# Turned q and k by plain transfers instead of VectorE copies, with the sync queue in program order

## The chip, the cores and the metric

The kernel runs on one core of a Trainium2 chip. The metric is the time of one execution on the device, in microseconds. A core has five engines that run side by side, each with its own in-order queue: TensorE (PE; matrix products, with a separate view of its weight loads, PEld), VectorE (DVE), ScalarE (ACT), GpSimd (POOL) and SyncE (SP). SP computes nothing here: it issues transfers. 16 DMA engines move the data of all queues. On-chip memory is SBUF; TensorE writes to PSUM.

## The reference

Causal attention with a learned decay, on a batch of 8, 8 heads, 576 positions, head size 64, followed by a low-rank mix over positions and a two-layer channel mix.

```python
scores = scale * np.matmul(q, k.transpose(0, 1, 3, 2))
cum = np.cumsum(np.maximum(s, 0.0), axis=-1)
bias = -(cum[:, :, :, None] - cum[:, :, None, :])
scores = np.where(causal, -1000000000.0, scores + np.minimum(bias, 0.0))
attn = softmax(scores)                       # over the last axis
x = np.matmul(attn, v)                       # heads side by side: [8, 576, 512]
h = xt @ U @ V                               # xt: x transposed to [8, 512, 576], rank 32
u = x + h.transpose(0, 2, 1)
out = u + np.maximum(u @ w_ch1, 0.0) @ w_ch2 # 512 -> 2048 -> 512
```

## The kernel before

The 64 heads are worked off as 32 pairs, four pairs to a batch (`NP` = 32, `PB` = 4). The main loop runs over pairs `n` from 8 to 33, with `b, hp = divmod(n, PB)`. One iteration prepares the score operand of pair n+1, computes the scores of pair n (`scores`, L429), and the weighted values of pair n-1 (`values`, L493). Between these steps, `step_fill` puts pieces of the channel mix of earlier tokens (`chanmix`, L662 and L720), so that TensorE always has something to do. In the second pair of each batch (hp = 1) the sequence mix of the batch before runs as well (`seqmix`, L522 to L592): its additions on VectorE (L547) read `xT`, the transposed x of all four pairs of that batch.

The score operand of a pair lies in one of three slots in turn (`slot_of(n)`): 68 partitions, 64 for the head size and four for the decay, and for each of the two heads 576 columns of q and 576 of k. The four decay rows come from DRAM (`rows_of`, two transfers on SP, L302).

For batches 0 to 3, q and k are transposed by TensorE. From batch 4 on (`ZB` = 4) this is done by transfers: `load_pairs` brings q and k in by GpSimd's queue (L121), `turn_pair(n)` (L358) is one DMA transpose on SP from there to a landing place of 128 partitions, 64 for each head of the pair, and `part_pair(n)` copies each half to the slot with VectorE (L366). There are three landing places in turn. `part_pair` has two yields, after each of which the loop puts a piece of fill.

SP issues all transposes and sends in one queue: the turns (L358), the rows (L302), the transposes of x that `values` issues after a pair's second head (`xT`, L510), the transpose of u for the channel mix (`u_sd`, L1026), and the sends of finished quarters of the output (L744). In batches 4 to 7 the planner of the framework chooses SP's order by its own estimates, as it does for VectorE and ScalarE. TensorE's and GpSimd's queues keep the order in which the program was written: the last line of the kernel is `in_program_order(tc, traced, [E.Pool, E.PE])`, which ties each instruction to the one before it on its engine.

An x_sb write (L503) normalises the values of one head; the second of a pair makes that pair's x ready for its transpose. `first_sums` and `total` (L698) and the additions of `outputs_by_quarters` (L734) are the rest of VectorE's work here, with the masks (L373).

Of the kernel before, what the change touches and what calls it, by code (L numbers as in the profile page):

```python
# [19 lines left out]
def in_program_order(tc, first, engines):  # L20

    traced, last = tc.nc.cur_bb.bb.instructions, {}
    for ins in list(traced)[first:]:
        if ins.engine not in engines:
            continue
        prev = last.get(ins.engine)
        if prev is not None:
            tc.add_manual_dep(
                ins,
                prev.name,  # L30
                mybir.DependencyInfo(
                    mybir.DependencyClass.NoSync, mybir.DependencyReason.DATA
                ),
                reason="in_program_order",
            )
        last[ins.engine] = ins
# [3 lines left out]
def kernel(  # L40
# [12 lines left out]
    nc = tc.nc  # L53
    traced = len(nc.cur_bb.bb.instructions)
    E = mybir.EngineType
    B, H, S, D = q.shape
# [7 lines left out]
    NP = BH // 2  # L64
    PB = NP // B
# [5 lines left out]
    ZB = 4  # L71
# [13 lines left out]
    def pwork():  # L85
        return ps_w.tile([128, 512], FP32, tag="w", name="pwork")
# [23 lines left out]
    def by_pairs(b):  # L110
        return qk_sd[b % 2][:TR, :QK].rearrange(
            "p (hp c t two d) -> p hp c t two d", hp=PB, c=2, t=RT, two=2
        )
# [4 lines left out]
    def load_pairs(b):  # L118
        for h in range(H):
            for c, src in enumerate((q, k)):  # L120
                nc.gpsimd.dma_start(  # L121
                    out=by_pairs(b)[:, h // 2, c, :, h % 2, :],
                    in_=src[b, h].rearrange("(t p) d -> p t d", p=TR),
                )
# [51 lines left out]
    def v_slot(b):  # L176
        return v_slots[b % 3 if b < 3 else 2 - b % 2]

    def load_v(b, parts=range(5)):
        vt = v_slot(b)  # L180
        if 0 < b < 3:
            init_v(nc.gpsimd, vt)
        for t in parts:
            rows_t = 128 if t < 4 else 64
            nc.gpsimd.dma_start(  # L185
                out=vt[:rows_t, t, :, 0:D],
                in_=v[b, :, ds(t * 128, rows_t), :].rearrange("h p d -> p h d"),
            )
# [10 lines left out]
    def slot_of(n):  # L199
        return slots[n % NSLOT if n < 2 * PB else (n + 1) % 3]  # L200
# [28 lines left out]
    for n in range(PB):  # L229
        for hh in range(2):  # L230
            nc.sync.dma_start(
                out=slots[n][D:KA, hh, 0 : 2 * S],
                in_=rows[2 * n + hh : 2 * n + hh + 1].rearrange("n r c s -> n r (c s)"),
# [3 lines left out]
    for r, n_r, c in ((0, 3, 1), (3, 1, 0)):  # L237
        nc.sync.dma_start(
            out=rows_hbm[ds(r, n_r), ds(2 * PB, BH - 2 * PB)].rearrange("r n s -> n r s"),
            in_=rows[2 * PB :, ds(r, n_r), c, :],  # L240
# [59 lines left out]
    def rows_of(n):  # L300
        for r, n_r, c in ((0, 3, 1), (3, 1, 0)):
            nc.sync.dma_start(  # L302
                out=slot_of(n)[ds(D + r, n_r), :, ds(c * S, S)],
                in_=rows_hbm[ds(r, n_r), ds(2 * n, 2)],
            )
# [47 lines left out]
    def landing(n):  # L353
        return landings[(n - ZB * PB) % 3]

    def turn_pair(n):
        b, hp = divmod(n, PB)
        nc.sync.dma_start_transpose(  # L358
            out=landing(n).rearrange("p (a m) -> p a m", m=TR),
            in_=by_pairs(b)[:, hp].rearrange("p c t two d -> p (c t two d)"),  # L360
        )

    def part_pair(n):
        rows_of(n)
        for hh in range(2):
            nc.vector.tensor_copy(slot_of(n)[0:D, hh, 0 : 2 * S], landing(n)[ds(hh * D, D)])  # L366
            yield

    def mask(dst, n_tiles, w, on_pool=False):
        if on_pool:  # L370
# [105 lines left out]
    def place(j, i):  # L476
        if i == j:
            return 128 * j if j < 4 else 1536
        return {0: 512, 1: 1024, 2: 1344, 3: 960}[j] + 128 * (i - j - 1)

    def values(n, pT):
        b, hp = divmod(n, PB)
        if hp == 0:
            x_of[b] = work.tile([128, PB, 5, 128], BF16, tag="x_sb", name="x_sb")
            if b >= FT:
                xT_of[b] = work.tile([128, 4, 640], BF16, tag="xT", name="xT", bufs=1)
        x_sb, vt = x_of[b], v_slot(b)
        for hh in range(2):
            h = 2 * hp + hh
            po = pwork()[:, : 5 * (D + 1)].rearrange("p (i d) -> p i d", i=5)  # L490
            for i in range(5):
                for j in range(i + 1):
                    nc.tensor.matmul(  # L493
                        po[:, i, :],
                        lhsT=pT[:, hh, ds(place(j, i), 128)],
                        rhs=vt[:, j, h, :],
                        start=(j == 0),
                        stop=(j == i),
                        skip_group_check=True,
                    )  # L500
            rec = work.tile([128, 5, 1], FP32, tag="rec", name="rec", bufs=4)
            nc.vector.reciprocal(rec, po[:, :, D : D + 1])  # L502
            nc.vector.tensor_tensor(  # L503
                x_sb[:, hp, :, ds(hh * D, D)],
                po[:, :, 0:D],
                rec.to_broadcast([128, 5, D]),
                op=ALU.mult,
            )
            if hh == 1 and b >= FT:
                nc.sync.dma_start_transpose(  # L510
                    out=xT_of[b][:, hp, :].rearrange("p (t m) -> p t m", t=5),
                    in_=x_sb[:, hp, :, :].rearrange("p t d -> p (t d)"),
                )
            yield
# [564 lines left out]
    def step_fill():  # L1079
        pace[0] += pace[1]  # L1080
        if pace[0] < 16:
            return
        pace[0] -= 16
        if NG - 3 in expanded and not ps_tail:
            return
        while fill:
            if next(fill[0], fill) is not fill:
                return
            fill.pop(0)

    def run(gen):
        for _ in gen:
            step_fill()
# [5 lines left out]
    def fill_with(n):  # L1099
        per, pace[1] = pace[1], 16  # L1100
        for _ in range(n):
            step_fill()
        pace[1] = per


    def pT_of(n):
        if n < PB + 3:
            return pTs[n % 2] if n % PB < 2 else pT_early[n % PB - 2]
        return pTs[(n + 1) % 2]

    def step(*gens):
        for gen in gens:
            next(gen, None)
# [85 lines left out]
    def load(b):  # L1199
        alloc_qk(b)  # L1200
        for h in range(0, H, 4 if b == 2 else H):
            load_qk(b, h, 4 if b == 2 else H)
# [38 lines left out]
    pace[1] = 11  # L1241
    for n in range(2 * PB, NP + 2):
        b, hp = divmod(n, PB)
        if hp == 0 and b + 1 < ZB:
            load(b + 1)
        if hp == (1 if b >= ZB else PB - 1) and ZB <= b + 2 < B:
            load_pairs(b + 2)
        if ZB * PB <= n + 3 < NP:
            turn_pair(n + 3)
        mixing = seqmix(b - 1) if hp == 1 and b > FT else iter(())  # L1250
        if b == B:
            fill_with(3)
            for _ in range(3):
                step(mixing)
                fill_with(2)
        if n > 2 * PB and n + 1 < NP:
            for at, _ in enumerate((transposes if n + 1 < ZB * PB else part_pair)(n + 1)):
                step_fill()
                if at == 0:
                    step(mixing)  # L1260
        if 2 * PB + 1 < n < NP:
            for at, _ in enumerate(scores(n, pT_of(n))):
                step_fill()
                if at == 1:
                    step(mixing)
        for _ in mixing:
            fill_with(1)
        if hp == 1 and FT < b < B:
            fill.append(chanmix(b - 1))
            pace[1] = 12 if b < 6 else 10  # L1270
        if 2 * PB < n <= NP:
            run(values(n - 1, pT_of(n - 1)))
        if hp == 0 and 2 <= b < B - 1:
            load_v(b + 1)
    pace[1] = 16
# [36 lines left out]
    while fill:  # L1312
        step_fill()
    in_program_order(tc, traced, [E.Pool, E.PE])


# [28 lines left out]
```

## Time and profile before

| what | value |
|---|---|
| median of 3 runs | 357.68 us (357.58 to 359.25) |
| the profiled execution: its own time | 359.33 us |
| the profiled execution: its span | 357.6 us |
| TensorE busy | 343.6 us (96%) |
| VectorE busy | 264.4 us (74%) |
| L366, copies from a landing place in qk_sd | 20, 475 ns each |
| L366, copies from the landing place `turned` | 12, 478 ns each |
| DMA queue of SP (q1) | 61,640 packets, 22.83 MB, 36.0% of 16 engines' span |
| DMA queue of GpSimd (q0) | 101,744 packets, 18.45 MB, 80.7% |
| granted TensorE clock | 1.00 throughout |

The page shows one profiled execution; the span is what its instructions cover, and the execution's own time is 1.7 us longer. "L547" is line 547 of the kernel. In the timeline a bracket after an instruction tells how long its engine was idle ahead of it and what released it. Matmuls are pipelined, so a group's length is somewhat more than its share of the engine. A packet's time includes the time in which its engine also served another queue, so the shares of the queues can sum to more than one.

### The profile page before, as it was taken

What the parts mean: (1) busy time and instruction counts of PE and PEld (TensorE: products, weight loads), DVE (VectorE), ACT (ScalarE), POOL (GpSimd) and SP (SyncE); (2) the same over time, 40 slices, a digit from 0 to 9 for tenths busy, and PEclk for the clock granted to TensorE, in tenths of its full rate; (3) what the DMA queues carried; (4) which work ended last, traced back from release to release, by engine and by line L of the source; (5) the groups of instructions that cost most, each with busy time, mean ns of one, the idle gap of its engine ahead of it and who ended that gap; (6) DMA issues with size and microseconds to landing.
All of it is one profiled execution on the core that took longest, in us unless ns stands there. A gap on an engine that the chain in (4) does not pass through costs nothing.

```text
span 357.6 us, 9219 instructions
## 1 busy us (share of the span) xinstructions
PE 343.6 (96%) x3770; PEld 247.9 (69%) x3770; DVE 264.4 (74%) x584; ACT 207.6 (58%) x314; POOL 112.6 (31%) x158
## 2 busy tenths in 40 slices
PE   7999999999998999999999997899899999999996
PEld 3685656665587657775678565776588558888885
DVE  8686776779789849883798465983788779676774
ACT  4786965847762577348833874347752554675710
POOL 8897274447356603850366040000000000000000
PEclk9999999999999999999999999999999999999999
DMA  6999999999999999999599999472033525010022
GB/s 100 163 193 203 177 187 121 146 144 97 192 101 171 162 168 88 167 176 159 72 120 160 204 118 90 73 163 57 0 57 83 115 30 120 29 60 31 29 90 88
DMA packets 163713, 42.06 MB, mean 118 GB/s; under 512 B 148312, under 2 KB 162040, under 8 KB 163672
## 3 DMA queue, kind: packets, MB, share of 16 engines
q0 software_dynamic: 101744, 18.45, 80.7%
q1 hardware_dynamic: 61640, 22.83, 36.0%
q8 instruction: 29, 0.48, 0.6%
q10 hardware_dynamic: 288, 0.20, 0.2%
q14 instruction: 12, 0.10, 0.1%
HBM read 37.25 MB, written 9.70 MB: 131 GB/s over the span
## 4 chain that ended last, share of the span: by engine, by line
PE 77%; DVE 12%; ACT 5%; DMA 4%; issue 2%; POOL 0%; DVEq 0%; ACTq 0%; POOLq 0%
PE pwork L662 22%; PE pwork L720 12%; PE quarter L720 9%; PE pscore L429 9%; PE pwork L493 7%; PE parts L950 6%; PE pwork L681 3%; DVE uT L547 3%; DMA xT<-x_sb 2%; ACT pT L447 2%; PE pwork L322 2%; DVE slot L345 2%; DVE o_sb L734 2%; DVE slot L698 2%; ACT hT L1039 1%
## 5 line engine op out<-in xcount | busy, mean ns | idle before, releaser
L662 PE MATMUL pwork<-uT,w_sb 128*128 128x512 bf16 x432 | 106.6, 379 | 1.1 <-ACT hT L1039 0.9
L447 ACT ACTIVATE pT<-pscore 128x1024 bf16<-128x1024 f32 x56 | 56.5, 1031 | 52.7 <-PE pscore L429 52.3
L1039 ACT ACTIVATE hT<-pwork 128x512 bf16<-128x512 f32 x108 | 65.4, 610 | 37.1 <-PE pwork L662 36.3
L662 PEld LDWEIGHTS <-w_sb 128*128 128x128 bf16 x448 | 38.7, 98 | 38.0 <-issue 1.3
L429 PE MATMUL pscore<-slot 68*128 68x320 bf16 (+1 forms) x500 | 55.4, 246 | 0.6 <-ACT hT L447 0.3
L185 POOL DMA_DIRECT2D v_slot<-in_v_dram x40 | 33.8, 860 | 67.9 <-PE pwork L493 57.6
L429 PEld LDWEIGHTS <-slot 68*128 68x128 bf16 x564 | 41.8, 97 | 18.2 <-issue 1.2
L373 DVE TENSOR_TENSOR pT<-pT,keep 128x512 bf16<-128x512 bf16 (+1 forms) x81 | 28.5, 353 | 31.7 <-ACT pT L447 28.7
L720 PEld LDWEIGHTS <-hT 128*128 128x128 bf16 x496 | 46.7, 98 | 7.5 <-issue 0.8
L493 PEld LDWEIGHTS <-pT 128*128 128x128 bf16 x870 | 32.5, 97 | 10.2 <-issue 4.4
L493 PE MATMUL pwork<-v_slot,pT 128*128 128x65 bf16 x870 | 35.8, 193 | 3.8 <-DVE uT L547 3.1
L503 DVE TENSOR_TENSOR x_sb<-pwork,rec 128x320 bf16<-128x320 f32 x64 | 31.2, 489 | 1.5
L459 ACT ACTIVATE pT<-pscore 128x1024 bf16<-128x1024 f32 x29 | 30.4, 1047 | 2.6 <-PE pscore L429 2.4
L720 PE MATMUL pwork<-w_sb,hT 128*128 128x256 bf16 x240 | 30.1, 273 | 0.3 <-DVE o_sb L734 0.3
L345 DVE COPY slot<-pwork 64x576 bf16<-64x576 bf16 x30 | 24.1, 803 | 7.2 <-PE pwork L322 6.8
L121 POOL DMA_DIRECT2D qk_sd<-in_q_dram x32 | 23.8, 743 | 14.0 <-PE pwork L322 4.9
L720 PEld LDWEIGHTS <-slot 128*128 128x128 bf16 x256 | 24.1, 98 | 5.0 <-issue 1.9
L121 POOL DMA_DIRECT2D qk_sd<-in_k_dram x32 | 23.7, 740 | 5.7 <-DMA v_slot<-in_v_dram 1.8
L720 PE MATMUL pwork<-w_sum,slot 128*128 128x256 bf16 x160 | 20.1, 273 | 1.1 <-DVE o_sb L734 1.1
L720 PE MATMUL quarter<-w_sb,hT 128*128 128x256 bf16 x144 | 18.0, 273 | 0.3 <-DVE uT L547 0.3
L681 PE MATMUL pwork<-w_sb,hT 128*128 128x512 bf16 x64 | 16.3, 379 | 0.0
L502 DVE RECIPROCAL rec<-pwork 128x5 f32<-128x5 f32 x64 | 12.0, 189 | 5.4 <-PE pwork L493 5.0
(166 smaller groups left out, 513.7 us busy)
## 6 DMA issues: line engine op xcount, KB each, us to landing
out_dram<-o_sb SPq DMA_DIRECT2D x34, 256.0 KB
v_slot<-in_v_dram POOLq DMA_DIRECT2D x32, 128.0 KB, 7.7
w_sb<-in_moe_w_ch_dram POOLq DMA_DIRECT2D x4, 1024.0 KB, 13.3
qk_sd<-in_q_dram POOLq DMA_DIRECT2D x32, 72.0 KB, 6.0
qk_sd<-in_k_dram POOLq DMA_DIRECT2D x32, 72.0 KB, 5.9
qk_sd<-in_q_dram POOLq DMA_DIRECT2D x4, 288.0 KB, 12.4
qk_sd<-in_k_dram POOLq DMA_DIRECT2D x4, 288.0 KB, 11.5
qk_sd<-in_q_dram POOLq DMA_DIRECT2D x4, 144.0 KB, 5.2
```

The lines of the kernel that those rows point to most:

```text
L121: nc.gpsimd.dma_start(out=by_pairs(b)[:, h // 2, c, :, h % 2, :], in_=src[b, h].rearrange("(t p) d -> p t d", p=TR),)
L185: nc.gpsimd.dma_start(out=vt[:rows_t, t, :, 0:D], in_=v[b, :, ds(t * 128, rows_t), :].rearrange("h p d -> p h d"),)
L345: copies(n, hh, par)(in_turn[:, :, :, :, par], src.rearrange("p c t m -> p c m t"))
L373: nc.vector.tensor_tensor(dst, dst, keep[:, :, 0:w].to_broadcast([128, n_tiles, w]), op=ALU.min)
L429: nc.tensor.matmul(dst, lhsT=slot[0:KA, hh, ds(S + j * 128, 128)], rhs=slot[0:KA, hh, lo:hi], start=True, stop=True,)
L447: nc.scalar.activation(pT[:, hh, 0:1024], near, EXP, scale=scale)
L459: nc.scalar.activation(pT[:, :, 1024:1536], mid.rearrange("p (a b) -> p a b", a=2), EXP, scale=scale)
L493: nc.tensor.matmul(po[:, i, :], lhsT=pT[:, hh, ds(place(j, i), 128)], rhs=vt[:, j, h, :], start=(j == 0), stop=(j == i), skip_group_check= ...
L503: nc.vector.tensor_tensor(x_sb[:, hp, :, ds(hh * D, D)], po[:, :, 0:D], rec.to_broadcast([128, 5, D]), op=ALU.mult,)
L662: nc.tensor.matmul(f1, lhsT=w1_sb[:, kt, ds(nf * 128, 128)], rhs=u[:, kt, :], start=(kt == 0), stop=(kt == 3),)
L720: nc.tensor.matmul(acc[:, i, :], lhsT=a[:, kt, ds(i * 128, 128)], rhs=b[:, kt, :], start=(begin and i == 0 and kt == 0), stop=(kt == HF - ...
L1039: nc.scalar.activation(hT[:, nf, :], f1, RELU)
```

## The change

`part_pair` no longer copies with VectorE: each half of the landing place goes to its half of the slot by a plain transfer on SP, both issued together, and the two yields follow. `turn_pair(n + 3)` is moved from the top of the iteration to below `values(n - 1)`, which is where the transpose of x is issued; in the program it now stands behind that. From the iteration in which n is 12 (batch 3) on, SP's queue keeps the order of the program, as TensorE's and GpSimd's do.

In each iteration SP's queue thus holds, in this order: the rows and the two plain transfers of pair n+1, the sends and the transpose of u that fall into the iteration, the transpose of x of pair n-1, the turn of pair n+3.

```diff
     def part_pair(n):
         rows_of(n)
         for hh in range(2):
-            nc.vector.tensor_copy(slot_of(n)[0:D, hh, 0 : 2 * S], landing(n)[ds(hh * D, D)])
-            yield
+            nc.sync.dma_start(out=slot_of(n)[0:D, hh, 0 : 2 * S], in_=landing(n)[ds(hh * D, D)])
+        yield
+        yield
...
     for n in range(2 * PB, NP + 2):
         b, hp = divmod(n, PB)
+        if n + 4 == ZB * PB:
+            turning = len(nc.cur_bb.bb.instructions)
         if hp == 0 and b + 1 < ZB:
             load(b + 1)
         if hp == (1 if b >= ZB else PB - 1) and ZB <= b + 2 < B:
             load_pairs(b + 2)
-        if ZB * PB <= n + 3 < NP:
-            turn_pair(n + 3)
...
         if 2 * PB < n <= NP:
             run(values(n - 1, pT_of(n - 1)))
+        if ZB * PB <= n + 3 < NP:
+            turn_pair(n + 3)
...
     in_program_order(tc, traced, [E.Pool, E.PE])
+    in_program_order(tc, turning, [E.SP])
```

Lines from L366 on move down by one in the changed kernel, and those below L1243 by up to three (the score matmuls L429 are L430 there, the transposes of x L511, the sends L745).

## Prediction

> **What bounds the kernel now.** I read the page's first part first. TensorE is busy 343.6 of 357.6 us, VectorE 264.4, so an edit off TensorE pays only where TensorE stands still and that edit's work is what it stands still for.
>
> ```profile
> span 357.6 us, 9219 instructions
> PE 343.6 (96%) x3770; PEld 247.9 (69%) x3770; DVE 264.4 (74%) x584; ACT 207.6 (58%) x314; POOL 112.6 (31%) x158
> ```
>
> Next the windows, cut where the change acts. Columns: window, length, then busy time (and count) of PE, weight loads, DVE, ACT, POOL, the granted clock, and the DMA share summed over the queues.
>
> ```profile
> 108.00:118.00 10.00, 9.10 (x112) 7.41 (x111) 9.91 (x24) 1.69 (x3) 4.68 (x7) 1.00 1.81 176
> 118.00:140.00 22.00, 22.00 (x228) 13.39 (x226) 15.22 (x37) 17.45 (x28) 5.89 (x9) 1.00 1.15 140
> 140.00:150.00 10.00, 9.61 (x111) 7.94 (x109) 9.06 (x21) 3.82 (x5) 8.61 (x12) 1.00 2.39 143
> 150.00:172.00 22.00, 22.00 (x235) 15.02 (x234) 13.45 (x34) 13.65 (x21) 6.99 (x10) 1.00 1.65 167
> 172.00:187.00 15.00, 14.35 (x173) 10.85 (x171) 14.34 (x34) 7.88 (x13) 9.27 (x12) 1.00 1.27 88
> 187.00:212.00 25.00, 25.00 (x270) 17.17 (x268) 15.71 (x41) 15.90 (x25) 7.51 (x11) 1.00 1.51 167
> 212.00:230.00 18.00, 14.39 (x169) 11.34 (x168) 13.29 (x31) 6.26 (x10) 3.18 (x4) 1.00 1.31 75
> 230.00:246.00 16.00, 16.00 (x189) 11.77 (x187) 11.79 (x29) 10.89 (x17) 0.00 (x0) 1.00 0.67 134
> ```
>
> TensorE idles only around the four sequence mixes (windows 1, 3, 5 and 7), and in the first three of these DVE is full. In the other 85 us TensorE has no gap at all: DVE time removed there is worth nothing. The seventh window, from the timeline (start, length, engine, line, idle time ahead in brackets):
>
> ```profile
> 211.86 2.62 SPq L358 DMA_TRANSPOSE qk_sd<-qk_sd  x1
> ...
> 214.58 1.23 SPq L510 DMA_TRANSPOSE xT<-x_sb  x1
> ...
> 223.29 0.76 DVE L547 TENSOR_TENSOR uT<-pwork,xT 128x192 bf16<-128x192 f32 x2 [3.27 <-DMA xT<-x_sb]
> ...
> 224.10 0.61 PE L493 MATMUL pwork<-v_slot,pT 128*128 128x65 bf16 x15 [2.83 <-DVE uT L547]
> ```
>
> Pair 23's x was written at 212.82, but SP was still issuing a q, k transpose; the x transpose went out behind it and its data queued behind that one's too. VectorE waited 3.27 us and TensorE, behind it, 2.83.
>
> **Part one: 32 copies leave VectorE.** 20 x 475 ns + 12 x 478 ns (the L366 groups) = 15.2 us of DVE. What is on the path: in 108 to 118 two copies (0.71 + 0.56) stand straight ahead of the mix's L547, and TensorE's gaps there are 0.28 + 0.24 + 0.30 us, behind L547 and o_sb: 0.82 gained. In 140 to 150 two copies (0.91) stand ahead of L547: the gap of 0.39 gained. In 172 to 187 four copies (1.80): 0.65 gained. Sum 1.9 us; the other 13 us lie beside a full TensorE.
>
> **Part two: x ahead of q, k.** xT of pair 23 would go out at 212.9 rather than 214.58, with no transpose ahead of it, and land some 4 us earlier than its measured 222.3. Then L547's last adds follow the earlier ones at 220.0. What is late next is VectorE's own backlog: from 220.0 it needs the 3.5 us that it took from 223.29 to 226.78 to reach the o_sb add that TensorE waits for (0.78 us at 226.83); TensorE would want it at 226.05 - 2.83 = 223.2 and get it at 223.5. So 2.83 + 0.78 - 0.3 = 3.3 us gained. Bounds: 0 if xT is still caught by the v loads that GpSimd issues at 210.97, 3.6 at most. Total gain 5.2 us; between 1.9 and 5.5.
>
> **Part three: what the plain transfers make late.** Before, a slot's copy ran as soon as its last reader was done (pair 16's at 109.34, pair 13's last score matmul at 109.11) and was wanted three pairs later. Now SP issues in program order: x transpose of pair m-3, turn of pair m+1, two row loads and two plain transfers of pair m, then whatever sends and u_sd stand there. Nothing of pair m's operand goes out before x of pair m-3 is written, and TensorE, in program order itself, stands at scores(m) until it has landed, with all fill matmuls queued behind. The time allowed is from the end of the second x_sb write (L503) of pair m-3 to the first score matmul of m (L429), both in the timeline. For m = 16 to 31 it is 7.8, 8.9, 12.6, 7.6, 8.3, 8.8, 12.9, 7.7, 7.3, 8.9, 15.8, 6.6, 7.2, 8.1, 13.0, 6.1 us. (The x write at 153.74 + 0.48 = 154.22 and scores at 161.77 give pair 19's 7.6.)
>
> The plain transfer from SBUF to SBUF has no row in this trace. For its issue I take 0.53 us, that of an output send (out_dram, 0.53; a row load 0.57); bounds 0.25 to 1.2. For its data, packets of 2304 B took 93 to 360 ns in the packet records of SP's queue; 64 over 16 engines are four in a row, 0.4 us alone, 1.4 at most. The landing I take from turns in the quiet stretch: issued at 207.33 for 1.32, its last packet ended at 210.16, 1.5 us after. Quiet chain: xT 1.23 + turn 1.31 + rows 2 x 0.5 + first copy 0.53 + gaps 0.4 + landing 1.3 = 5.8 us. The second copy lands 0.7 later and is wanted 1.3 later (second head). 5.8 is under every allowance, so in quiet stretches the copies are hidden; the cover is thin, 0.8 us at pair 27 and 1.4 at pair 28. Pair 31's chain has no turn: 4.4 against 6.1.
>
> In the stretches where GpSimd's loads of q, k, v run (142 to 160, 176 to 202, 211 to 222), the same rows are longer: xT issues in 1.6, the turn in 2.2 to 2.85, and counted off in ring order (640 packets of 256 B to an xT, 1152 to a turn; all 50,176 are accounted for) the data of the xT issued at 154.25 ended at 160.01, 5.8 us later, against 2.3 for one issued at 208.78. The ring keeps its order, so the copies come after that. Pair 19: xT's data to 160.0, a send 0.9, the turn 2.4, rows 0.3, first copy 0.6: 164.2, wanted at 161.77, less about 0.5 for VectorE writing x sooner: **2.0 us lost**. Pair 23 likewise, from x at 189.67: xT data to about 195.3, turn 2.7, rows 0.3, copy 0.8, so 199.1 against 197.39: 1.7, less 0.5 for x sooner, **1.2 lost**. Pair 24 follows it with three sends ahead: 0.3. Pair 16, the first, has u_sd (4.6 us of issue) in front of xT(13): 0.2. Pairs 18, 22 and 26 are issued in loaded stretches too, but have 13 to 16 us. After u_sd, pairs 21 and 25 should just make it. With half a microsecond for those not exactly hit: **4.2 us**. Bounds: below, 0 (only if the copies land with the chain of the quiet rows; a wait cannot give time back); above, 10 (rival two).
>
> TensorE also gets 16 more semaphore waits in its queue; such an instruction shows 17 to 28 ns on SP: 0.2 us taken, 0.5 at most. u_sd goes out later than before by up to 15 us in two batches (156.54 before, about 168 now), but its first reader, the o_sb add at 181.17, still finds it landed by 176. Sends go out later by some 4 us and nobody waits for them but o_sb's three buffers.
>
> How much slower the loaded ring is, the rows give unevenly: an xT's data take 0.94 us alone and 2.65 or 3.57 loaded, a turn's 1.62 alone and 2.4 to 3.5 loaded; I took 2.65 and 2.4 at pair 19. The Trainium skill, DMA: Bandwidth & Descriptors, section Queues, rings and completion order, speaks against the change here: a DMA engine takes turns packet by packet between the queue rows that have work, so a plain transfer put on SP's row gets no way past GpSimd's loads. Worked out from that rule as an even turn between two rows (an estimate: every transfer twice its quiet time), pair 19's chain would lose 2.7 us instead of 2.0, pair 23's 1.0 instead of 1.2, and the sum would come to -0.3 us.
>
> **Sum.** -5.2 + 4.2 + 0.2 = -0.8 us. On the profiled execution (span 357.6, its own time 359.33, 1.7 outside the span) that is 356.8 and 358.5; that execution lay 1.65 above the median of the runs shown, so against the median: 357.68 - 0.8 = 356.9 us. About 0.5% (1.8 us) is what a measurement of this kernel can tell from no change; faster means below 355.9, slower above 359.5.
>
> **Rivals.** One: the copies stay hidden in the loaded stretches as well, because there are now fewer turns packed together there (before, those at 178.42 and 182.86 followed one another) and xT leads. Then at most 3 us of stalls: 352.5 to 355.9, say 354.3. For it: TensorE's gaps are shown, VectorE's copies stand ahead of them. Against: the 5.8 us landing.
>
> Two, slower: SP itself becomes the pace in the loaded stretches. Its issue per pair is there xT 1.6 to 2.2, turn 2.2 to 2.85, rows 1.0 to 1.3, copies 1.1, a send 0.55, a quarter of u_sd's 5 us, gaps 0.7: 8.4 to 9.9 us, against a pair's 7.5. It decides once that sum exceeds 7.5 for several pairs running, so that the lateness adds up rather than being caught up. Pairs 19, 20, 22, 23, 24 and 26 at 1 to 2 us each, 10 us with the rest; less 5.2: 362.5. For it: SP has no slack when u_sd comes, and the allowance was 20 us before. Against: the pair with the mix in it gives 5 us back each batch.
>
> Three: the reordering does not bring xT forward in time (SP late by u_sd and copies when x of pair 23 is written); 3.3 us are not gained, 4.2 still lost: 359.8 to 360.5. That the copies leave VectorE at all is certain from the built queues: 32 fewer instructions on VectorE, 32 more transfers on SP, TensorE's order unchanged.
>
> **How the numbers follow.** Forecast (stalls and gains within 1.8 us of each other) 0.34, range 355.9 to 359.5; rival one 0.30; rivals two 0.29 and three 0.07, together 0.36 slower. For eight in ten, a third of rival one (below 353.5) and a third of rival two (above 362.8) are left out.
>
> **What would show it.** Right: no L366 on VectorE; the 3.27 us wait for xT gone; TensorE idle at L430 (scores) released by a DMA of L366, some 2 us near 162 and over 1 near 198, and nowhere after 230; windows 3 and 5 full for TensorE. Wrong: waits for L366 at nearly every pair (rival two), also in the quiet 118 to 140 or 204 to 212, would say that the plain transfer's landing or its issue is longer than its nearest rows; none at all is rival one; xT still waited for near 220 is rival three.

## The result: slower, by 2.7%

The changed kernel takes 367.12 us (median of six runs, 364.80 to 369.04) against 357.63 us for the kernel before in the same comparison: a ratio of 1.0273, 95% interval 1.0220 to 1.0326. The forecast was 356.9, the range 353.5 to 362.8: the time lies above it. The profiled execution of the changed kernel took 368.98 us, its span is 367.3. Ratios, here and below, leave out executions more than 1.5% above the fastest of their kernel, and medians do not, so a ratio is not quite the quotient of two medians.

The first part of the page of the changed kernel answers to the one shown of before:

```profile
span 367.3 us, 9170 instructions
PE 346.9 (94%) x3735; PEld 249.7 (68%) x3770; DVE 250.4 (68%) x552; ACT 208.9 (57%) x314; POOL 112.4 (31%) x158
```

VectorE is relieved as intended (264.4 to 250.4 us). TensorE is idle for 20.4 us instead of 14.0, and its busy time has grown by 3.3 us although its work is the same. The same windows as before, of the changed kernel, with the same columns:

```profile
118.00:140.00 22.00, 19.78 (x164) 11.06 (x165) 9.49 (x25) 15.87 (x25) 5.46 (x8) 0.92 1.11 153
150.00:172.00 22.00, 19.01 (x187) 13.31 (x187) 11.86 (x28) 9.24 (x13) 8.06 (x12) 0.92 1.60 199
187.00:212.00 25.00, 20.55 (x216) 15.45 (x215) 14.67 (x35) 8.62 (x13) 10.76 (x15) 0.95 1.94 171
212.00:230.00 18.00, 17.84 (x183) 11.02 (x185) 8.74 (x22) 14.04 (x23) 4.21 (x5) 0.98 1.22 141
```

The stretches that were full (22.00, 22.00, 25.00) now hold 2.2 to 4.5 us of idle TensorE, and the granted clock, 1.00 throughout before, is 0.92 to 0.95 in them (0.98 in the last row). As forecast, no wait for xT is left. What TensorE waits for there stands in the changed kernel's waits (total, times, longest):

```profile
PE pscore L430 <- DMA slot<-turned: 4.4, 2, 2.9
PE pscore L430 <- DMA slot<-qk_sd: 3.8, 2, 2.9
PE pscore L430 <- DMA slot<-rows_hbm: 2.0, 1, 2.0
```

These 10.2 us are five waits at the first score matmul of a pair: pair 15 (2.00, at 127.09), pair 19 (2.88, at 166.67), pair 22 (1.54, at 197.28), pair 23 (2.86, at 207.82) and pair 29 (0.92, at 259.47). The timeline shows three of them with what SP issued ahead (start, length, engine, line):

```profile
119.12 2.02 SPq L358 DMA_TRANSPOSE turned<-qk_sd  x1
121.19 1.46 SPq L302 DMA_DIRECT2D slot<-rows_hbm  x2
...
127.09 0.74 PE L430 MATMUL pscore<-slot 68*128 68x128 bf16 x6 [2.00 <-DMA slot<-rows_hbm]
...
156.36 1.79 SPq L511 DMA_TRANSPOSE xT<-x_sb  x1
...
158.95 1.53 SPq L358 DMA_TRANSPOSE qk_sd<-qk_sd  x1
160.57 1.38 SPq L302 DMA_DIRECT2D slot<-rows_hbm  x2
162.00 1.13 SPq L366 DMA_DIRECT2D slot<-turned  x2
...
166.67 0.60 PE L430 MATMUL pscore<-slot 68*128 68x128 bf16 x6 [2.88 <-DMA slot<-turned]
...
184.77 2.83 SPq L358 DMA_TRANSPOSE qk_sd<-qk_sd  x1
187.70 1.37 SPq L302 DMA_DIRECT2D slot<-rows_hbm  x2
189.12 1.50 SPq L366 DMA_DIRECT2D slot<-turned  x2
...
197.28 0.62 PE L430 MATMUL pscore<-slot 68*128 68x128 bf16 x6 [1.54 <-DMA slot<-turned]
```

Pair 15's operand is still made by TensorE; only its rows are late, two row loads of 1.46 us of issue that now stand behind the turn of pair 16, whose data end at 124.79. Pair 19 is the one that was forecast. Pair 22's copies are issued at 189.12, but by the packet records the turn ahead of them on the ring (the row of packets that all of SP's transfers share, worked off in order) ends at 192.70 and their own packets run from 194.59 to 197.35: eight microseconds from issue to landing.

Behind three of the five waits the clock is halved. One-microsecond windows of the changed kernel behind pair 15's wait (PE busy first, the granted clock in the third column from the end):

```profile
126.00:127.00 1.00, 0.00 (x0) 0.10 (x1) 0.00 (x0) 0.00 (x0) 0.00 (x0) 1.00 1.94 215
127.00:128.00 1.00, 0.91 (x7) 0.52 (x7) 0.00 (x0) 0.14 (x1) 0.00 (x0) 0.71 1.35 265
128.00:129.00 1.00, 1.00 (x4) 0.39 (x3) 0.08 (x1) 0.88 (x1) 0.00 (x0) 0.50 1.18 258
129.00:130.00 1.00, 1.00 (x7) 0.62 (x6) 0.34 (x1) 0.43 (x1) 0.00 (x0) 0.50 1.14 247
130.00:131.00 1.00, 1.00 (x5) 0.41 (x4) 0.00 (x0) 0.74 (x2) 0.00 (x0) 0.59 0.55 111
```

**The running lag.** TensorE's queue is the same in all kernels here: 3770 weight loads in one order. The start of the k-th load in one trace minus its start in another therefore tells how far one kernel lags behind the other at that piece of work. The table is worked out in this way from the starts in the traces, against a second profile of the kernel before (below, an execution of 355.38 us), whose time scale is on the left. Kernels by their labels in the experiments.

```
 at   before,1st  after   e10    e5     e6    e14    e4    e15
110      0.45     0.09   0.09   0.23   0.13   0.07   0.14  -0.13
114      0.57    -0.74  -0.75  -0.61  -0.70  -0.77  -0.69  -0.96
126      0.57     1.44   1.78   2.02  -0.75   0.99   1.28  -1.01
130      0.57     3.04   1.78   2.02  -0.75   0.99   1.28  -1.01
146      0.57     3.04   1.93   2.02  -0.75   0.99   2.46  -1.01
150      0.57     2.43   1.32   1.41  -1.36   0.38   1.85  -1.62
162      0.57     5.46   4.86   1.41  -1.36   2.22   1.86  -1.62
166      0.57     7.14   4.86   1.41  -1.36   2.22   1.86  -1.62
182      0.57     7.14   4.86   1.41  -1.36   2.22   1.88  -1.62
186      0.58     6.28   3.99   3.42  -0.22   1.36   1.02  -2.48
190      0.58     7.99   4.73   3.42  -0.22   1.36   1.47  -2.48
198      0.58    11.01   7.27   3.42  -0.22   2.08   1.47  -2.48
202      0.58    12.68   8.94   3.42  -0.22   2.08   1.47  -2.48
222      3.57    12.68   8.93   5.69   1.82   2.08   3.06  -2.49
226      3.94    12.67   8.93   6.06   2.20   2.08   3.06  -2.49
250      3.94    13.34   9.37   6.06   2.20   2.08   3.29  -2.49
350      3.95    13.55   9.57   6.28   2.42   2.30   3.51  -1.07
```

Read the column of the changed kernel downwards. It gains 0.83 us at 110 to 114, 0.61 at 146 to 150 and 0.86 at 182 to 186, at the mixes: 2.30. It loses at pair 15 (2.19, then 1.60 by the clock), pair 19 (3.04, then 1.68), pair 22 (1.71), pair 23 (3.02, then 1.67), and 0.66 and 0.22 later: 10.84 by waits and 4.95 by the clock. 10.84 + 4.95 - 2.30 = 13.5, which is the 13.55 at the end.

The profiled execution has more of the clock's share than most. Each half-clock stretch in it is 3.413 us long. The six executions of the changed kernel had a granted clock of 0.985, 0.995, 0.989, 0.989, 0.986 and 0.991 over their spans; what is missing from 1, times the span, over half of 3.413 us, gives an estimate of 3, 1, 2, 2, 3 and 2 such stretches. Their times go with it: 364.80 us with one, 366.20, 366.81 and 367.42 with two, 368.98 and 369.04 with three.

### The profile page after: what moved, and what is told of

Read it like the earlier page. It is cut to its first block, busy times and chain, and to the rows that moved or that the text cites. A ratio compares the mean times of both kernels' runs of the same rounds, so it can differ in the third digit from the quotient of the medians.

```text
span 367.3 us, 9170 instructions
## 1 busy us (share of the span) xinstructions
PE 346.9 (94%) x3735; PEld 249.7 (68%) x3770; DVE 250.4 (68%) x552; ACT 208.9 (57%) x314; POOL 112.4 (31%) x158
## 4 chain that ended last, share of the span: by engine, by line
PE 35%; DMA 29%; issue 19%; POOL 9%; DVE 4%; ACT 2%; SPq 1%; POOLq 0%; DVEq 0%
DMA qk_sd<-in_q_dram 11%; PE quarter L721 9%; PE pwork L663 8%; DMA qk_sd<-in_k_dram 8%; DMA v_slot<-in_v_dram 6%; PE parts L951 5%; PE pwork L721 5%; POOL qk_sd L121 4%; DMA slot<-qk_sd 3%; PE pscore L430 3%; POOL v_slot L185 2%; PE pwork L494 2%; POOL qk_sd L134 2%; DVE uT L548 1%; PE pwork L951 1%
## 5 line engine op out<-in xcount | busy, mean ns | idle before, releaser
L663 PE MATMUL pwork<-uT,w_sb 128*128 128x512 bf16 x405 | 107.9, 389 | 1.9 <-ACT hT L1040 0.4
L448 ACT ACTIVATE pT<-pscore 128x1024 bf16<-128x1024 f32 x56 | 56.5, 1030 | 57.2 <-PE pscore L430 57.1
L430 PE MATMUL pscore<-slot 68*128 68x320 bf16 (+1 forms) x500 | 57.5, 251 | 10.7 <-DMA slot<-turned 4.4
L663 PEld LDWEIGHTS <-w_sb 128*128 128x128 bf16 x448 | 39.7, 100 | 39.5 <-issue 4.4
L430 PEld LDWEIGHTS <-slot 68*128 68x128 bf16 x564 | 42.3, 99 | 30.4 <-issue 6.3
L460 ACT ACTIVATE pT<-pscore 128x1024 bf16<-128x1024 f32 x29 | 30.2, 1041 | 3.2 <-PE pscore L430 3.1
L682 PE MATMUL pwork<-w_sb,hT 128*128 128x512 bf16 x58 | 15.0, 378 | 0.4 <-issue 0.2
```

What stands on the lines that cost most here:

```text
L430: nc.tensor.matmul(dst, lhsT=slot[0:KA, hh, ds(S + j * 128, 128)], rhs=slot[0:KA, hh, lo:hi], start=True, stop=True,)
L448: nc.scalar.activation(pT[:, hh, 0:1024], near, EXP, scale=scale)
L460: nc.scalar.activation(pT[:, :, 1024:1536], mid.rearrange("p (a b) -> p a b", a=2), EXP, scale=scale)
L663: nc.tensor.matmul(f1, lhsT=w1_sb[:, kt, ds(nf * 128, 128)], rhs=u[:, kt, :], start=(kt == 0), stop=(kt == 3),)
```

## The experiments

The kernel before measured 355.65, 356.10, 355.96 and 355.95 us in the four comparisons that follow.

**The copies back on VectorE, SP's order kept (e1).**

```diff
-            nc.sync.dma_start(out=slot_of(n)[0:D, hh, 0 : 2 * S], in_=landing(n)[ds(hh * D, D)])
-        yield
-        yield
+            nc.vector.tensor_copy(slot_of(n)[0:D, hh, 0 : 2 * S], landing(n)[ds(hh * D, D)])
+            yield
```

> The changed kernel with the VectorE copies of q, k put back: only SP's program order (from batch 3) and the moved turn are left of the change. Theory (the change loses its time where TensorE stands at scores behind operands that went out late, in program order on SP's one queue, and in the 3.3 us at half clock that follow the long ones of these stalls): row loads still go out in that order, so the 2.0 us at pair 15 and the half clock behind it (1.6 us) stay, the stalls released by the plain transfers (2.9, 1.5, 2.9, 0.9 us) shrink to under 3 us in all; xT of pair 23 is forward (3.3 gained), VectorE's 1.9 is not gained: 357 to 361 us. Rival A (the plain transfers cost what they cost by their landing, whatever the order): the copies are gone, so 354 to 357. Rival B (the program order alone is the loss): 364 to 367, with stalls at scores near 167, 197 and 208 as before.

Measured: 392.84 us, ratio 1.1032 (1.0986 to 1.1078). No theory expected this. The waits of VectorE, and the timeline of the longest one:

```profile
DVE slot L366 <- DMA qk_sd<-qk_sd: 25.8, 10, 6.3
...
DVE slot L366 <- DMA turned<-qk_sd: 21.5, 6, 7.1
```

```profile
147.44 2.39 SPq L358 DMA_TRANSPOSE turned<-qk_sd  x1
...
155.46 0.45 DVE L366 COPY slot<-turned 64x1152 bf16<-64x1152 bf16 x1 [7.12 <-DMA turned<-qk_sd]
...
156.50 0.61 PE L567 MATMUL pscore<-V_sb,ux 32*128 32x512 bf16 x2 [6.08 <-DVE ux L537]
```

With SP in program order a turn goes out late, and VectorE stands in its own queue at the copy for 47.3 us in all; TensorE then waits for what VectorE has behind it (here the cast of ux). So SP's order and the VectorE copies do not go together, and this kernel cannot price the order alone.

**The plain transfers alone (e2).** The same edit the other way round, on the kernel before: the planner still chooses SP's order.

> The kernel before with its 32 VectorE copies as plain transfers on SP, and nothing else: no program order on SP, turns where they were. Theory: SP's queue then holds the copies where the planner has put them, each waiting for the last reader of its slot, and what stands behind them on SP (an x transpose, sends) waits too; copies wanted three pairs later are hidden if the planner puts them early, so few stalls at scores: 354 to 359. Rival A (the transfers' landing costs, whatever the order): stalls of 1.5 to 3 us at scores released by the copies at several pairs, 364 or more. Rival B (the program order is the loss): 353 to 356.

Measured: 374.07 us, ratio 1.0471 (1.0401 to 1.0541). Slower than the whole change, but not as rival A has it: TensorE does not wait for the copies. From this kernel's timeline:

```profile
146.57 0.49 SPq L366 DMA_DIRECT2D slot<-turned  x1
147.17 1.59 SPq L511 DMA_TRANSPOSE xT<-x_sb  x1
...
154.89 1.09 DVE L548 TENSOR_TENSOR uT<-pwork,xT 128x320 bf16<-128x320 f32 x3 [6.29 <-DMA xT<-x_sb]
```

The x transpose issued behind a copy at 147.17 is used at 154.89, and TensorE stands 6.01 us behind VectorE. Rival B (the order is the loss) falls here too: without the order it is worse. Each part alone is worse than both together. What it loses is xT late at three mixes:

```profile
DVE uT L548 <- DMA xT<-x_sb: 16.2, 3, 7.0
```

In the first of them x was written at 141.11; SP had a turn, two row loads and two copies to issue before its transpose.

**The copies on ScalarE's queue (e3).**

```diff
-            nc.sync.dma_start(out=slot_of(n)[0:D, hh, 0 : 2 * S], in_=landing(n)[ds(hh * D, D)])
+            nc.scalar.dma_start(out=slot_of(n)[0:D, hh, 0 : 2 * S], in_=landing(n)[ds(hh * D, D)])
```

> The changed kernel with the two plain transfers of a pair issued by ScalarE instead of SP: another queue, so their data are not behind xT and the turn of the same pass, and SP's issue is 1.1 us shorter. Theory: the waits for the copies at pairs 19, 22 and 23 mostly go (under 2 us left in all) with the half clock behind them; the wait for the rows at pair 15 (2.0 and its 1.6 of clock) stays; ScalarE's exp is late by 1.1 us a pair at places: 355 to 360. Rival A (landing costs whatever the queue): stalls at scores released by the copies as long as now, 365 to 369. Rival B (the program order is the loss): since the copies still stand behind the same rows in the same order, 364 to 367.

Measured: 393.60 us, ratio 1.1016 (1.0932 to 1.1099). All three expectations missed, for the reason of e1 on another engine. ScalarE's waits:

```profile
ACT pT L448 <- DMA qk_sd<-qk_sd: 9.1, 1, 9.1
ACT pT L448 <- DMA slot<-rows_hbm: 8.5, 1, 8.5
ACT pT L460 <- DMA qk_sd<-qk_sd: 8.1, 1, 8.1
```

ScalarE's exponentials (L448, L460) stand behind a transfer that it may not issue before the turn has landed. Of the three engines, SP is the one that has nothing of TensorE's next steps behind the copy except transfers.

**Rows and copies one pair earlier (e5).**

```diff
-            for at, _ in enumerate((transposes if n + 1 < ZB * PB else part_pair)(n + 1)):
+            for at, _ in enumerate(transposes(n + 1) if n + 1 < ZB * PB else range(2)):
...
+        if ZB * PB <= n + 2 < NP:
+            drain(part_pair(n + 2))
...
-        if ZB * PB <= n + 3 < NP:
-            turn_pair(n + 3)
+        if ZB * PB <= n + 4 < NP:
+            turn_pair(n + 4)
```

> The changed kernel with rows and copies going out one pair earlier in the program (those of pair n+2 after TensorE's work of pass n, the turn of n+4): same queue, same order, same number of transfers, some 7.5 us more cover each. Theory: stalls at scores released by the copies go, with the half clock behind two of them; rows(15) stays behind a turn (2.0 and 1.6 of clock at most): 353 to 357. Rival A (the transfers' landing costs, whatever the cover; they take the ring from x and rows): 362 to 368, with xT or the rows late instead. Rival B (program order is the loss): stalls go too, but x transposes stand behind copies that wait for their slot's last reader: 358 to 364, waits for xT at the mixes.

Measured: 361.94 us, ratio 1.0162 (1.0110 to 1.0214); granted clock 1.00 in the profiled execution, 0.99 in the other three. Its waits:

```profile
PE pwork L494 <- DVE uT L548: 5.0, 3, 2.7
PE pscore L430 <- DMA slot<-rows_hbm: 2.5, 1, 2.5
```

No score matmul waits for a copy any more: with a pair more of cover the same 32 transfers on the same queue are hidden, as the theory has it. But the time is 5 to 9 us above the theory's: the wait for the rows of pair 15 stays, and waits for xT at the mixes have come in (2.7 and 2.1 us). That is what rival A foresaw, whose 362 to 368 begins where this kernel landed, and rival B as well. The next kernels go after the two.

**The same, and SP's order from n = 15 on (e6).**

```diff
-        if n + 4 == ZB * PB:
+        if n + 1 == ZB * PB:
```

> The kernel with rows and copies one pair earlier, and SP's program order beginning three passes later, so that the rows of pair 15 no longer stand behind the turn of pair 16. Theory (the loss is operands late on SP's one queue): the 2.5 us at scores for those rows goes, nothing else changes: 358 to 360 us. If the plain transfers cost what they cost by taking the ring from x (xT waits of 2.7 and 2.1 us in the kernel with rows and copies one pair earlier), it stays above the kernel before by 2 to 4 us: that is the same number, and the VectorE twin of this kernel tells it apart. Rival (order alone is the loss): no change from 362.

Measured: 358.75 us, ratio 1.0069 (1.0047 to 1.0092), 3.2 us below e5 and within the 358 to 360 of the theory: the rows of pair 15 no longer stand behind a turn. What is left, from its timeline:

```profile
185.53 0.62 PE L494 MATMUL pwork<-v_slot,pT 128*128 128x65 bf16 x15 [1.84 <-DVE uT L548]
...
222.35 0.61 PE L494 MATMUL pwork<-v_slot,pT 128*128 128x65 bf16 x15 [1.89 <-DVE uT L548]
```

**Its twin with VectorE copies (e11).** The edit of e1 on e6.

> The twin of the kernel with rows and copies one pair earlier and the order beginning later: the copies on VectorE again, all else alike, x still ahead of q, k. Theory (what made the kernel with VectorE copies in the changed order lose 37 us was VectorE standing in its own queue for a turned block that had not landed, and one pair more of cover takes that away): 353 to 360 us, no VectorE wait for a turn over 1 us. If the plain transfers themselves are a cost by the ring, this one is 2 to 4 us below its twin; if they are a gain (VectorE's 1.9 us), it is 1 to 2 us above it. Rival (the order alone is the loss): 365 or more.

Measured: 375.62 us, ratio 1.0555 (1.0502 to 1.0608). The theory's claim that one pair more of cover frees VectorE fell: VectorE still waits 20.2 us for turns, TensorE 5.28 and 6.11 us behind it at two mixes.

**The turn ahead of x again (e10).** `turn_pair(n + 3)` back at the top of the pass, all else as changed.

> The changed kernel with the turn back at the top of the pass, ahead of x: only 'x ahead of q, k' is undone; plain transfers and program order stay. Theory (lateness at scores adds up from what stands between the x transpose and the copies on SP): the turn's 1.3 to 2.8 us leave that stretch, so the stalls at scores for copies (2.9, 1.5, 2.9, 0.9 us) shrink to under 3 us in all and the half clock behind two of them goes (3 us less); the wait for rows at pair 15 stays or shrinks; against it xT is later by a turn, 0 to 3 us at the mixes: 358 to 364. Rival (x ahead is worth 3.3 us or more, and the copies' landing is what costs): 367 to 371.

Measured: 366.80 us, ratio 1.0333 (1.0252 to 1.0414), no different from the changed kernel's 367.12. Its waits at the scores:

```profile
PE pscore L430 <- DMA slot<-turned: 3.6, 2, 3.0
PE pscore L430 <- DMA slot<-qk_sd: 3.3, 3, 2.4
PE pscore L430 <- DMA slot<-rows_hbm: 2.4, 1, 2.4
```

9.3 us, against 10.2, and no wait for xT although x goes out behind the turn. "x ahead of q, k" moves nothing that can be measured here; the intervals of the two ratios overlap, and with one half-clock stretch each, by the granted clock, the two kernels take 365.02 and 365.32 us (e10) and 364.80. The theory's 358 to 364 missed; the time is at the foot of the rival's 367 to 371, but the wait for xT that the rival needs is not there. In this profile only one of the waits has half clock behind it (1.67 us by the lag, against 4.95 in the changed kernel's); that is 3.3 of the 4.0 us by which its last row in the table is lower. Two of its other executions had a granted clock of 0.981, about four such stretches, and took 368.27 and 370.12 us.

**The kernel before once more (e8).**

> The kernel before once more, unchanged, for a second profile: its times lie between 355.1 and 359.3 us, and the profile from which the gain of 3.3 us by x ahead of q, k was read is of an execution at 359.33. If pair 23's waits for xT (3.27 us on VectorE, 2.83 on TensorE) belong to the kernel, they are in this profile too, within 1 us; if they belong to that one execution, this profile shows less than 1.5 us there and a time near 356.

Measured: 355.38 us, span 353.7. The line of the first profile, and the one that answers to it in the second:

```profile
PE pwork L493 <- DVE uT L547: 3.1, 2, 2.8
```

```profile
PE pwork L493 <- DVE uT L547: 0.2, 1, 0.2
```

The wait for pair 23's xT does not belong to every execution of the kernel; in how many it stands was not profiled. In the lag table it is the step from 0.58 to 3.94 in the first column.

**Without the copies (e14).** The transfers of L366 left out, so that the scores from batch 4 on read what their slot held before.

```diff
-        for hh in range(2):
-            nc.sync.dma_start(out=slot_of(n)[0:D, hh, 0 : 2 * S], in_=landing(n)[ds(hh * D, D)])
```

> The changed kernel without any copy of q, k to the score operands from batch 3 (left out: the plain transfers; scores then read what their slot held before; turns, rows and SP's order stay). It splits the lateness at scores into what comes ahead of the copies (xT, turn, rows) and the copies' own issue and landing (1.1 to 1.5 us and some 2 us after). Theory (both share it): the wait for rows at pair 15 with its half clock stays (3.8 us), the others shrink to 0 to 1.5 us each: 358 to 362. If the copies' own landing were all, 357.5 to 358.5; if what is ahead of them were all, 364 or more.

Measured: 358.15 us, ratio 1.0063 (1.0042 to 1.0084). Its waits at the scores (L428 there):

```profile
PE pscore L428 <- DMA slot<-rows_hbm: 3.9, 3, 1.7
```

The time lies where two of the expectations overlap and does not decide between them; the waits do. Of the 10.2 us, 3.9 are what stands ahead of the copies (the rows themselves are late, at pairs 15, 19 and 23: 1.65, 1.68 and 0.57), and 6.3, by subtraction, the copies; without these the granted clock is 1.00.

**Without GpSimd's q, k of batches 6 and 7 (e4).**

```diff
-        if hp == (1 if b >= ZB else PB - 1) and ZB <= b + 2 < B:
+        if hp == (1 if b >= ZB else PB - 1) and ZB <= b + 2 < 6:
```

> The changed kernel without GpSimd's loads of q, k for batches 6 and 7 (left out: those batches then turn older data; the loads of v and all else stay). In the changed kernel TensorE stands 1.54 us at the scores of pair 22 and 2.86 at those of pair 23, with 1.7 us more in half clock, in the stretch where the loads of batch 6 run (about 183 to 206). Theory (the ring is slow for xT, turn and copies because GpSimd's loads run): these go, pairs 15, 19 and 29 and their half clock stay: 360 to 362.5. Rival (SP's order and issue alone make them late, whatever the load): both stalls stay: 366 to 368.

Measured: 357.71 us, ratio 1.0057 (1.0036 to 1.0078), 2.3 us below the expected range: batch 6 is loaded earlier than the expectation says, so the loads left out are also those beside pair 19, and its wait went as well (no step at 162 in the lag table). Left are:

```profile
PE pscore L430 <- DMA slot<-turned: 2.7, 3, 1.4
PE pscore L430 <- DMA slot<-rows_hbm: 1.9, 1, 1.9
```

The order and the issue are unchanged here; without these loads beside them they cost 5 us of waits instead of 10.2, and no half clock in the profiled execution. They stand at pairs 15, 16 and 25 (1.87, 1.01 and 1.44 us), of which the last two did not wait in the changed kernel. Taking away the copies (e14) or the loads (e4) each leaves 0.6% of the 2.7%: a wait is what is left over above the cover, and the half clock comes only where it fills more than half of a window (last section).

**GpSimd's loads later (e12), and the control (e13).** On e6 and on the kernel before: `load_pairs` at the end of the second pass of a batch, `load_v` at the end of the third.

```diff
-        if hp == (1 if b >= ZB else PB - 1) and ZB <= b + 2 < B:
-            load_pairs(b + 2)
...
-        if hp == 0 and 2 <= b < B - 1:
+        if hp == (1 if b >= ZB else PB - 1) and ZB <= b + 2 < B:
+            load_pairs(b + 2)
+        if hp == 2 and 2 <= b < B - 1:
             load_v(b + 1)
```

> The kernel with rows and copies one pair earlier and the order beginning later (358.75 us; TensorE still stands 1.84 and 1.89 us at the mixes near 186 and 222 behind an xT that shares the rings with GpSimd's loads), with these loads moved: q, k of batch b+2 at the end of the second pass of a batch instead of its beginning, v of batch b+1 at the end of the third pass instead of the first, so that none is under way while the last xT of a batch lands. Theory (what is left of the loss is xT late on rings loaded by GpSimd): both waits go, what VectorE gains without its copies (0.83, 0.61, 0.86 us at three mixes) remains: 353 to 356, at or 1 to 2 us below the kernel before. Rival (the plain transfers' data on SP's ring are what delays xT): the waits stay: 357 to 359. If q, k or v then come too late for their own users, a wait for them appears and the time rises.

> The kernel before with the same two moves of GpSimd's loads and nothing else: the control for the kernel with later loads. The second profile of the kernel before has no xT wait, the first (an execution 4 us longer) has one of 2.83 us, so the moves have little to remove in the typical execution: 354 to 357 us, with a smaller spread. If it gains as much as the kernel with later loads does, that one owes its time to the loads, not to the change.

Measured: e12 356.04 us, ratio 0.9982 (0.9956 to 1.0008); e13 356.84, ratio 1.0021 (1.0004 to 1.0037). The wait at 185 is gone, as the theory has it; the one at the last mix is not, since GpSimd ran ahead of the other engines and issued the load of that v at 209.50:

```profile
221.40 0.73 PE L494 MATMUL pwork<-v_slot,pT 128*128 128x65 bf16 x15 [2.09 <-DVE uT L548]
```

**The last load of v held back (e15), and the control (e16).** On e12, and the same hold on the kernel before.

```diff
         if hp == 2 and 2 <= b < B - 1:
+            if b == B - 2:
+                held = work.tile([1, 1], BF16, tag="held", name="held", bufs=1)
+                nc.gpsimd.tensor_copy(held, xT_of[b][0:1, 0, 0:1])
             load_v(b + 1)
```

> The kernel with later loads, and GpSimd's load of v for the last batch held back (a copy of one element of the x transpose of pair 24 ahead of it in GpSimd's queue) until the last xT of batch 5 has landed; in the kernel with later loads GpSimd issued it at 209.50, and TensorE stood 2.09 us at 221.40 behind that xT, with 1.2 us more in half clock. Theory (xT is late there because v's load shares the ring): wait and half clock go, and what VectorE gains without its copies, 2.3 us by the running lag, is left: 352.5 to 354.5, 0.5 to 0.9% below the kernel before. Rival (the plain transfers ahead of xT on SP's ring delay it): the wait stays, 355.5 to 357. Rival (SP's order has another cost still hidden): 355 and above without a wait at 221.

> The kernel before with the same hold on the last load of v and nothing else: the control. In the typical execution of the kernel before xT is not waited for, so 354.5 to 356.5, with the slow executions (to 359.3, 2.8 us of wait behind xT near 224 in the one profiled) gone. If it lands with the kernel with the hold (352.5 to 354.5), that one owes its time to the hold.

Measured: e15 356.04 us, ratio 0.9999 (0.9976 to 1.0021); e16 355.64, ratio 0.9980 (0.9959 to 1.0001). The theory's 352.5 to 354.5 us missed. In the profiled execution of e15 (354.42, its shortest) the wait at 221 is gone, for the theory and against the plain transfers as its cause, and up to 250 the kernel is 2.49 us ahead. Then 1.2 us are lost at the mix near 252:

```profile
252.03 0.63 PE L494 MATMUL pwork<-v_slot,pT 128*128 128x65 bf16 x15 [1.02 <-DVE uT L548]
```

These additions read the x transpose of pair 27. Its x was written at 241.39, but on SP a turn, the transpose of u and a pair's rows and copies went first:

```profile
242.27 3.35 SPq L1027 DMA_TRANSPOSE u_sd<-uT  x1
...
248.09 1.26 SPq L511 DMA_TRANSPOSE xT<-x_sb  x1
```

In the second profile of the kernel before, where the planner orders SP, this transpose is issued at 243.91, and its x was written at 243.88. That speaks for the last rival (SP's order has another cost still hidden, 355 and above); no run tests it. The median is 1.6 us above the profiled execution, with a granted clock of 1.00 in ten of the twelve; what the others lose was not profiled and stays open. No version here beats the kernel before.

## Why the prediction was wrong, step by step

**Part one held.** 1.9 us forecast at the first three mixes (0.82, 0.39, 0.65); measured 0.83, 0.61, 0.86, together 2.30, in every kernel of the table whose copies left VectorE, as far as the mix was not waiting for xT. (In e6 and e5 the third gain is hidden by such a wait.)

**Part two failed.** "3.3 us gained" by x ahead of q, k was read from a wait that the first profile shows and the second (e8) does not. That execution took 359.33 us; the prediction noted that it lay 1.65 us above the median, and still carried its wait into the sum against the median. Its size was read rightly: in the first column of the table it is 3.94 - 0.58 = 3.36 us. The failed step is taking it for a cost of the kernel. With the turn put back ahead of x (e10) nothing waits for xT either, and the time is the same.

**Part three was the right mechanism, at less than half its size.** The forecast's 4.2 us of waits at the scores measured 10.84 by the lag (10.2 by the waits). By its own list:

- Pair 15 was not on it (2.19 measured). The 16 operands listed were those that the plain transfers make; the rows of a pair before them, which the order moves behind a turn as well, were not followed.
- Pair 22 was dismissed, with its 12.9 us allowed (1.71 measured). Pairs 18 and 26, dismissed with it, did hold, and so did 20, 21, 24 and 25 (no wait over 0.3 us).
- Pairs 19 and 23 were named with 2.0 and 1.2 us (3.04 and 3.02). The term that failed is what comes behind the turn's data: forecast 0.9 and 1.1 us for the rows and the first copy. The packet records show the turn's data ending at 164.37 and 205.16 and the operand landed at 166.67 and 207.82: 2.3 and 2.7 us; for pair 22 it was 4.6. The 128 packets of a pair's two copies run into one another and take 1.4 to 3.1 us.
- "Nowhere after 230" failed at pair 29, by 0.66 us. Issue was sized rightly: 588 ns per plain transfer in the median, 530 forecast.

The even turn between rows of the Trainium skill (DMA: Bandwidth & Descriptors, Queues, rings and completion order), weighed in the prediction as an estimate, put pairs 19 and 23 at 2.7 and 1.0 us; measured 3.04 and 3.02. It is nearer at pair 19 and does not give pair 23.

**A term was missing.** 4.95 us of the loss are TensorE at half clock behind the waits in the profiled execution, and about two such stretches of 1.6 to 1.7 us in the typical one. The prediction had the clock in its windows, at 1.00, and no step asked what a new idle stretch does to it. Waits priced at their own length were priced at two thirds of their cost there (10.84 of 15.79 us).

**The rivals.** One (all hidden) fell. Two comes nearest in time (362.5), but not in mechanism: SP did not become the pace, for the pairs between the late ones do not wait, and lateness does not add up from pair 16 to 26. Three: xT is not late in the changed kernel. Together: gains of 5.2 us were forecast and 2.3 measured, waits of 4.2 and 10.8, clock of none and 4.95. That makes 13.5 instead of -0.8, one profiled execution against the other (368.98 and 355.38); between the medians (367.12 and 357.63) it is 9.5.

## What to carry to other kernels

A gain that is one engine's wait for a transfer has to be seen in a second execution before it goes into a sum. When an in-order queue is tied to the program, price the last transfer of each chain by the landing behind all that the ring carries ahead of it, and follow every other user of that queue from the point where the order begins, not only those that the change is about. And a wait of about two microseconds on TensorE may cost 1.2 to 1.7 us more in clock: shortening or splitting it can gain more than its length.

## What the runs showed of the hardware

**Half clock after less than a window of idleness.** In the clock record of the traces the half-clock stretches are 3.413 us long or a whole multiple (but for the last, which the end of the program cuts off), and begin whole multiples of 3.413 us after the clock's first rise in that execution: in the changed kernel at 127.41, 168.37 and 209.33, each 12 x 3.413 = 40.96 us after the last. Cutting the traces on that grid and taking TensorE's idle time in each window:

| kernel | idle in one window of 3.413 us | the next window |
|---|---|---|
| after, pairs 15, 19, 23 | 2.00, 1.76, 1.90 | half clock |
| e10 at 202 to 205; e12 at 218 to 222 | 2.02; 2.09 | half clock |
| e10 and e4 at 124 to 127; e6 at 183 to 186 and at 221 to 224 | 1.93 and 1.85; 1.84 and 1.80 | full clock |
| before, the 2.83 us wait, over two windows | 1.47 and 1.46 | full clock |
| e10, the 3.03 us wait, over two windows | 1.46 and 1.62 | full clock |

So it is not the length of a wait but how much of one window it fills, and a little over half is enough: from full clock, in all traces here, above 1.93 always, below 1.76 never, in between both. Each of the three half-clock windows of the changed kernel and the one of e10 cost 1.60 to 1.68 us by the lag; the one of e12 cost 1.2 (a lag of 3.3 us for a wait of 2.09). The Trainium skill, TensorE: Matmul & The Clock Gate, Part 1, What's actually happening, has the free-running window of 3413 ns, and half clock after at least one idle window, about 3.4 us; the runs agree on the window and differ on the condition, and the measurement decides. The changed kernel's executions spread by 4 us with the number of half-clock stretches in them, one to three by the granted clock; that this number differs because a wait falls differently on the grid is argued, not shown.

**A copy that waits holds whoever issues it.** The same 32 copies in the same SP order cost 9.5 us on SP's queue and some 37 or 38 on VectorE's or ScalarE's, though 15 us of work was all that they were for VectorE.
